# The second transform stage in four quarters of the array: a change to a spectral filter with two dense layers behind it

## The chip, the cores and the metric

The kernel runs on one core of a Trainium2 chip. What counts is the device time of one launch in microseconds (us), the median of several runs. The engines of the core: TensorE (PE; its weight loads are shown as PEld), VectorE (DVE), ScalarE (ACT), GpSimd (POOL, unused here) and SyncE (SP), which issues all transfers.

## The reference

A sequence of 3008 tokens with 256 channels, four batches, all float32, is filtered in the frequency domain and then goes through two dense layers:

```python
X = np.fft.rfft(x, axis=1)                       # x: (4, 3008, 256)
Y = X * (filt_r + 1j * filt_i)[None]             # (1505, 256)
x = np.fft.irfft(Y, n=3008, axis=1).reshape(12032, 256)
r = np.maximum(x @ w_in, 0.0); x = (r * r) @ w_out          # 2048 wide
g = x @ w_gate; silu = g / (1.0 + np.exp(-g))
out = (silu * (x @ w_val)) @ w_out2                          # 1536 wide
```

## The kernel before

**The transform** is split as 3008 = 64 x 47 (and uses the 24 + 24 real rows that 47 folds to). Stage A is a product with a 128 x 128 matrix ("psA", input "x0", "x1" or "xin", stored to the DRAM tensor s1 of its batch). Stages B and C work on 16 *slots* of a batch. A slot is 96 rows (two sets of 48) by 2 x 256 columns: stage B multiplies it by the 96 x 96 block matrix of two 48 x 48 transforms ("psB"), VectorE multiplies the result by the complex filter (lines 519, 524 twice, and 536, which adds the two parts "t1" and "t2"), stage C multiplies by the inverse block matrix ("psC"), ScalarE copies it out and it is stored to s2. Slot 0 is special: real and imaginary rows mix, and it needs four matrices for every product, over 256 columns each. Stage D ("psx", line 790) takes s2 back to tokens and is the entrance of the dense layers.

**Two ways of multiplying float32.** In batch 0, and in batch 1's stage A, matmuls take whole float32 operands (lines 645, 671, 678, 731, 790). Everywhere else both operands are split into two float32r parts and a product is three matmuls (`product`, lines 365 to 367: low x high, high x high, high x low); ScalarE makes the high part (a cast, line 353) and VectorE the low part (a subtraction, line 357). For stages B and C of batches 1 to 3 that means two splits per slot (`fsplit`), and the split matrices of slot 0 lie in DRAM ("sc") and are fetched per batch ("sp").

**Where the pieces run.** `first_ab` does batch 0 ahead of everything else, since nothing can start without it: stage A, stages B and C (`inverse`), batch 1's stage A, then stage D for the first 1024 tokens. Batches 1 to 3 are cut into steps by the generator `stages_ab`, one `yield` each, and a step is called now and then between the products of the dense layers (`side`). The dense layers ("psh", "pA" to "pC", "gA" to "gC", "vA" to "vC", "psg", "psv", and "acc" for the second product of a layer) are over 9,000 matmuls on 128 x 128 blocks over 416 to 512 columns.

**The order** of each engine's instructions is fixed when the program is built. Each step is handed to a `Plan` with an engine, a cost in us that its author wrote down, a rank (its place in the text plus a bias) and the tiles it uses; `emit` plays the steps through, takes on each engine the one that can begin first by these costs (the lower rank within 0.12 us), and gives tiles to buffers. `Buffers` gives its buffers in the order in which the tiles were declared, so that a tile that can't have one yet holds back those behind it; the ones marked loose don't keep that order. On the chip each engine then runs its list strictly in that order and waits where data isn't there yet. The pools that matter here: `pool_f`, 12 buffers of 2 KB a row for the inputs, filters, split parts and outputs of stages A to C; `pool_bank`, four banks of the matmul output memory; `pool_z`, 14 buffers of 4 KB a row, which hold batch 0's inputs "b0" and filters "f0".

Of the kernel before, what the change touches and what calls it, by code (L numbers as in the profile page):

```python
# [21 lines left out]
NQ = 16  # L22
# [20 lines left out]
def _constants():  # L43
# [34 lines left out]
    z = np.zeros((48, 48))  # L78

    def two(x, y):  # L80
        m = np.zeros((96, 96))
        m[:48, :48], m[48:, 48:] = x, y
        return m

    def quarter(i, j, x):
# [11 lines left out]
    mats = [  # L97
        two(t, t), two(ti, ti),
        two(rr, t), two(mr, z), two(rm, z), two(mm, t),
        two(irr, ti), two(imr, z), two(irm, z), two(imm, ti),  # L100
    ]
    cm = np.zeros((96, 10, 96), np.float32)
    for i, m in enumerate(mats):
        cm[:, i] = m
# [62 lines left out]
class Plan:  # L167
# [39 lines left out]
    def emit(self):  # L207
# [22 lines left out]
        def begin(s):  # L230

            at = base[s.i]
            for t in s.tiles:
                if t.slot is None:
# [3 lines left out]
                    best = min((b.free[k] for k in t.among), default=None)  # L238
# [59 lines left out]
def fft_conv_moe_kernel(ctx, tc, x, filt, amat, cmat, sgn, w1, w2, wg, wv, wo, out):  # L298
# [6 lines left out]
    plan = Plan()  # L305
    add = plan.add
# [3 lines left out]
    sc = dr.tile([96, 2, 8, 96], F32, name="sc", tag="sc")  # L310
# [11 lines left out]
    pool_f = Buffers(sb, "f", 12)  # L322
    pool_d = Buffers(sb, "d", 4)
    pool_sp = Buffers(sb, "sp", 1)
# [6 lines left out]
    ch = sb.tile([96, 2, 96], F32R, name="ch")  # L331
    cl = sb.tile([96, 2, 96], F32R, name="cl")
    sg = sb.tile([96, 2, NQ], F32, name="sg")
# [166 lines left out]
    def by_slot(s):  # L500
        return s.rearrange("(r e) n d -> r (e n) d", e=4)

# [6 lines left out]
    def filtered(p, f, ff, q, t1, t2, engine):  # L509


        def pv():
            return p.t[:96].rearrange("p (c d) -> p c d", c=2)

        def cd(t):
            return t.t[:96].rearrange("p (c d) -> p c d", c=2)

        dve(
            lambda: nc.vector.tensor_tensor(cd(t1), pv(), ff()[:, 0:1, :].to_broadcast([96, 2, D]), op=ALU.mult),
            [p, f], [t1],  # L520
        )
        for c in range(2):
            dve(
                lambda c=c: nc.vector.scalar_tensor_tensor(
                    cd(t2)[:, c, :], pv()[:, 1 - c, :], sg[:, c, q:q + 1], ff()[:, 1, :], op0=ALU.mult, op1=ALU.mult
                ),
                [p, f, "sg"], [(t2, c)], cost=0.42,
            )
        if engine == "POOL":
            add(  # L530
                "POOL", 1.45, lambda: nc.gpsimd.tensor_tensor(t1.t[:96], t1.t[:96], t2.t[:96], op=ALU.add),
                [t1, (t2, 0), (t2, 1)], [t1],
            )
        else:
            dve(
                lambda: nc.vector.tensor_tensor(t1.t[:96], t1.t[:96], t2.t[:96], op=ALU.add),
                [t1, (t2, 0), (t2, 1)], [t1],
            )

    def stages_ab(b):  # L540
# [22 lines left out]


        v1, v2 = by_slot(s1[b]), by_slot(s2[b])

        def slot_product(p, m, q, hi, lo, special):
            if q:
                product(
                    p, lambda: p.t[:96], ["ch"], lambda: (ch[:, m, :], cl[:, m, :]),  # L570
                    [hi, lo], lambda: (hi.t[:96], lo.t[:96]), 546,
                )
                return
            for c in range(2):
                for s in range(2):
                    product(
                        p, lambda c=c: p.t[:96, c * D:(c + 1) * D],
                        [special], lambda i=2 * c + s: (special.t[:, 0, i, :], special.t[:, 1, i, :]),
                        [hi, lo], lambda s=s: (hi.t[:96, s * D:(s + 1) * D], lo.t[:96, s * D:(s + 1) * D]),
                        256, start=s == 0, stop=s == 1,  # L580
                    )

        def load_special(m):
# [654 lines left out]
```

## Time and profile before

| | |
|---|---|
| median of 3 runs | 2275.01 us (2273.07 to 2275.43) |
| the profiled execution | 2271.08 us, of which the span of its instructions is 2269.3 us |
| TensorE, busy | 2244.5 us, 99% |
| VectorE, busy | 1712.0 us, 75% |
| ScalarE, busy | 1381.1 us, 61% |

The profile is one execution. A matmul's record is longer than its distance to the next one, since matmuls overlap at their ends; how long something occupies TensorE is read from start to start. Every name in a row ("psB", "fhi") is a tile with its buffer number left out; a tile that is written by one of several wrappers shows under the name that the helper gave it. A whole float32 matmul leaves two records.

### The profile page before, as it was taken

The numbers are of one execution on the slowest core, as the hardware profiler recorded it, in microseconds if no ns is written. First come the engines' busy times: TensorE is split into PE (matmuls) and PEld (weight loads), VectorE is DVE, ScalarE is ACT, GpSimd is POOL, SyncE is SP. The second block draws the span as 40 slices with busy tenths as digits, with TensorE's granted clock in tenths as the row PEclk, the third lists the DMA queues.
The fourth block names the chain that finished last, engine by engine and source line by source line (L and its number), as shares of the span: only waits on it lengthen the run. The fifth ranks groups of instructions, "written<-read, shape, count | busy, mean of one in ns | idle before, by whom it ended". The sixth has DMA issues, their size and how long they took to land.

```text
span 2269.3 us, 28911 instructions
## 1 busy us (share of the span) xinstructions
PE 2244.5 (99%) x10142; PEld 1855.8 (82%) x10142; DVE 1712.0 (75%) x2844; ACT 1381.1 (61%) x2464; POOL 0.2 (0%) x4
## 2 busy tenths in 40 slices
PE   6999999999999999999999999999999999999999
PEld 2688888888888887888888888888888888889889
DVE  3898898887678888667787787766776766767765
ACT  2788655565665656666566665655555655555655
POOL 0000000000000000000000000000000000000000
PEclk8999999999999999999999999999999999999999
DMA  9987768655765555656454555454454454445453
GB/s 287 361 284 258 251 238 278 214 187 194 241 206 164 165 175 187 209 200 218 158 164 141 188 184 167 166 179 163 153 172 131 156 180 160 160 153 169 153 190 135
DMA packets 201425, 439.03 MB, mean 193 GB/s; under 512 B 18080, under 2 KB 110496, under 8 KB 201280
## 3 DMA queue, kind: packets, MB, share of 16 engines
q1 hardware_dynamic: 201280, 437.18, 58.2%
q8 instruction: 80, 1.31, 0.2%
q14 instruction: 65, 0.53, 0.1%
HBM read 365.48 MB, written 71.63 MB: 193 GB/s over the span
## 4 chain that ended last, share of the span: by engine, by line
PE 96%; DMA 3%; ACT 0%; DVE 0%; issue 0%; SPq 0%; ACTq 0%
PE acc L365 13%; PE acc L367 13%; PE acc L366 13%; PE pA L365 3%; PE pA L366 3%; PE pA L367 3%; PE gA L365 3%; PE vA L365 3%; PE vA L367 3%; PE vA L366 3%; PE gA L366 2%; PE gA L367 2%; PE psx L790 2%; PE pC L365 2%; PE pC L367 2%; PE pC L366 2%
## 5 line engine op out<-in xcount | busy, mean ns | idle before, releaser
L367 PE MATMUL acc<-glo,ws 128*128 128x512 f32 (+2 forms) x1280 | 492.6, 385 | 0.0
L365 PE MATMUL acc<-ghi,ws 128*128 128x512 f32 (+2 forms) x1280 | 492.6, 385 | 0.0
L366 PE MATMUL acc<-ghi,ws 128*128 128x512 f32 (+2 forms) x1280 | 492.4, 385 | 0.0
L357 DVE TENSOR_TENSOR glo<-v,ghi 128x512 fp32r<-128x512 f32 (+2 forms) x438 | 291.8, 673 | 88.3 <-ACT ghi L353 83.9
L353 ACT CAST ghi<-v 128x512 fp32r<-128x512 f32 (+2 forms) x438 | 264.2, 610 | 125.0 <-DVE v L967 70.5
L365 PEld LDWEIGHTS acc<-ghi,ws 128*128 128x128 f32 x1280 | 240.2, 188 | 44.8
L367 PEld LDWEIGHTS acc<-glo,ws 128*128 128x128 f32 x1280 | 240.2, 188 | 44.8
L366 PEld LDWEIGHTS acc<-ghi,ws 128*128 128x128 f32 x1280 | 240.3, 188 | 44.5
L955 ACT COPY v<-pA 128x512 f32<-128x512 f32 (+2 forms) x240 | 138.3, 576 | 153.6 <-PE pA L367 149.4
L955 ACT COPY v<-vA 128x512 f32<-128x512 f32 (+2 forms) x198 | 114.2, 577 | 117.0 <-PE vA L367 112.3
L955 ACT COPY v<-gA 128x512 f32<-128x512 f32 (+2 forms) x198 | 114.1, 576 | 98.5 <-PE gA L367 95.2
L961 DVE TENSOR_TENSOR v<-vC,v 128x512 f32<-128x512 f32 (+2 forms) x132 | 89.6, 679 | 110.5 <-ACT v L955 109.6
L961 DVE TENSOR_TENSOR v<-pC,v 128x512 f32<-128x512 f32 (+2 forms) x160 | 108.3, 677 | 70.5 <-ACT v L955 40.7
L967 DVE SCALAR_TENSOR_TENSOR v<-v 128x512 f32<-128x512 f32 (+2 forms) x240 | 156.2, 672 | 2.4
L961 DVE TENSOR_TENSOR v<-gC,v 128x512 f32<-128x512 f32 (+2 forms) x132 | 89.5, 678 | 89.1 <-PE gC L367 74.3
L981 ACT ACTIVATE v<-v 128x512 f32<-128x512 f32 (+2 forms) x198 | 123.3, 623 | 50.5 <-DVE v L961 49.8
L987 DVE TENSOR_TENSOR v<-v 128x512 f32<-128x512 f32 (+2 forms) x198 | 133.0, 674 | 2.9
L357 DVE TENSOR_TENSOR glo<-r,ghi 128x512 fp32r<-128x512 f32 (+2 forms) x144 | 95.7, 676 | 4.9 <-ACT ghi L353 4.9
L353 ACT CAST ghi<-r 128x512 fp32r<-128x512 f32 (+2 forms) x144 | 88.4, 614 | 12.7 <-PE acc L366 9.2
L974 ACT ACTIVATE r<-pA 128x512 f32<-128x512 f32 (+2 forms) x80 | 47.0, 588 | 80.5 <-PE pA L367 79.9
L365 PE MATMUL pA<-z,wa 128*128 128x512 f32 (+2 forms) x240 | 93.0, 387 | 0.6 <-ACT v L955 0.6
L366 PE MATMUL pA<-z,wa 128*128 128x512 f32 (+2 forms) x240 | 92.3, 385 | 0.0
(224 smaller groups left out, 4735.7 us busy)
## 6 DMA issues: line engine op xcount, KB each, us to landing
wa<-dc SPq DMA_DIRECT2D x212, 512.0 KB, 3.5
ws<-ds SPq DMA_DIRECT2D x160, 512.0 KB, 4.4
wb<-db SPq DMA_DIRECT2D x212, 384.0 KB, 5.1
db<-po SPq DMA_DIRECT2D x20, 512.0 KB, 5.9
wa<-db SPq DMA_DIRECT2D x20, 512.0 KB, 4.7
dc<-po SPq DMA_DIRECT2D x20, 512.0 KB, 4.9
bin<-s SPq DMA_DIRECT2D x48, 192.0 KB, 5.6
fil<-in_filt SPq DMA_DIRECT2D x48, 192.0 KB, 5.5
```

Of the source, the lines that this page charges most:

```text
L353: act(lambda: nc.scalar.copy(fhi(), fsrc()), [src], [hi], n, psum, rank)
L357: lambda: nc.vector.tensor_tensor(flo(), fsrc(), fhi(), op=ALU.subtract), [src, hi], [lo], n, rank=rank
L365: nc.tensor.matmul(p, wl, mh, start=start, stop=False, skip_group_check=True)
L366: nc.tensor.matmul(p, wh, mh, start=False, stop=False, skip_group_check=True)
L367: nc.tensor.matmul(p, wh, ml, start=False, stop=stop, skip_group_check=True)
L790: nc.tensor.matmul(o.t[:, begin - n * w:end - n * w], x3[i // 5].t[:, i % 5, 128 * h:128 * h + 128], ai[:, first + begin - lo:first + end ...
L955: act(lambda: nc.scalar.copy(v.t[:, :w], p.t[:, :w]), [p], [v], w, True, URGENT)
L961: lambda: nc.vector.tensor_tensor(v.t[:, :w], p.t[:, :w], v.t[:, :w], op=ALU.add), [p, v], [v], w, rank=URGENT
L967: lambda: nc.vector.scalar_tensor_tensor(h.t[:, :w], h.t[:, :w], 0.0, h.t[:, :w], op0=ALU.max, op1=ALU.mult),
L974: act(lambda: nc.scalar.activation(h.t[:, :w], p.t[:, :w], AF.Relu), [p], [h], w, True, URGENT)
L981: lambda: nc.scalar.activation(t.t[:, :w], src.t[:, :w], AF.Silu), [src], [t], w, psum, URGENT if psum else 0
L987: lambda: nc.vector.tensor_tensor(g.t[:, :w], g.t[:, :w], src.t[:, :w], op=ALU.mult), [g, src], [g], w,
```

## The change

Two slots form a *pair*, eight pairs a batch. A pair's input is loaded so that the first set of 48 rows of both slots lies in rows 0 to 47 and the second in rows 64 to 111, the slots side by side in the columns; one instruction now multiplies 48 rows by a matrix of 64 columns in one quarter (64 x 64) of the array. `quarters` writes the four matmuls of a product, one per quarter, in turn: two row groups (output bank 0 and 1) times two column groups (output partitions 0 to 63 and 64 to 127). Each streams 512 columns of whole float32; for pair 0, which holds slot 0, the first quarter takes four matmuls over 256 columns instead. This is done in all four batches, so that the splits of stages B and C, the "sc" tensor and the "sp" tiles go. The outputs of a product lie in two banks, each of which is filtered on its own over 128 rows.

In batch 0 line 536's addition is left out (`added` is False): "t1" and "t2" both go into the product of stage C, which is then eight matmuls (for pair 0, fourteen). In batches 1 to 3 the addition stays.

Pair inputs and evicted pairs of all batches ("bin" in batches 1 to 3, "eb") share a new pool of two buffers, `pool_e`; `pool_f` goes from 12 to 9, and batch 1's "e1" moves to `pool_h`. A pair is loaded by two transfers of 192 KB, stored by two; a slot's filter comes in two pieces of 64 rows, 16 of them unused. The eleven matrices `cm` stay in a tile of their own, and the signs are loaded in four pieces and set out by two copies. The planner takes two tiles of one pool in one step into account.

The core of the diff:

```diff
-    cm = np.zeros((96, 10, 96), np.float32)
+    mats = [t, ti, rr, mr, rm, mm, irr, imr, irm, imm]
+    cm = np.zeros((128, 11, 64), np.float32)
     for i, m in enumerate(mats):
-        cm[:, i] = m
+        cm[:48, i, :48] = m
+    cm[64:112, 0, 16:] = t
+    cm[64:112, 1, :48] = ti
+    cm[16:64, 10, :48] = cm[80:, 10, :48] = ti
...
-    pool_f = Buffers(sb, "f", 12)
+    pool_f = Buffers(sb, "f", 9)
     pool_d = Buffers(sb, "d", 4)
-    pool_sp = Buffers(sb, "sp", 1)
+    pool_e = Buffers(sb, "e", 2)
...
+    def quarters(o, fo, fs, m, i, r):
+        def fn():
+            res, src = fo(), fs()
+            streams = []
+            for g in range(2):
+                for k in range(2):
+                    shift = m == 1 and k == 1
+                    rows, cols = slice(64 * g, 64 * g + (64 if shift else 48)), slice(64 * k, 64 * k + 64)
+                    last = len(src[k]) - 1
+                    q = []
+                    for c in range(2):
+                        for n, d in enumerate(src[k]):
+                            if i or g or k:
+                                if c == 0:
+                                    w = cm[rows, 10 if shift else m, :]
+                                    q.append((res[g][cols], w, d[rows], n == 0, n == last))
+                            else:
+                                for s in range(2):
+                                    w = cm[rows, 2 + 4 * m + 2 * c + s]
+                                    first = s == 0 and n == 0
+                                    q.append((res[g][cols, c], w, d[rows, s], first, s == 1 and n == last))
+                    streams.append(q)
+            while any(streams):
+                for q in streams:
+                    if q:
+                        p, w, d, start, stop = q.pop(0)
+                        nc.tensor.matmul(p, w, d, start=start, stop=stop, skip_group_check=True)
+        add("PE", (0.95 if i else 1.4) * (2 if len(r) > 4 else 1), fn, list(r) + ["cm"], o)
...
+    def inverse(b, i, ys):
+        o = [bank("psC") for _ in range(2)]
+        quarters(
+            o, lambda: [cd(p) for p in o], lambda: [[cd(y) for y in t] for t in ys], 1, i,
+            [y if n == 0 else (y, c) for t in ys for n, y in enumerate(t) for c in range(2 if n else 1)],
+        )
+        e = Tile(pool_e, [128, 2, 2, D], F32, "eb")
+        for j in range(2):
+            act(
+                lambda j=j: nc.scalar.copy(e.t[:, j].rearrange("p c d -> p (c d)"), o[j].t), [o[j]], [(e, j)], psum=True
+            )
...
-        for q in range(NQ):
-            pair = step_b(q)
+        ready = [("s1", b, g) for g in range(NG)]
+        for i in range(NP):
+            xb = Tile(pool_e, [128, 2, 2, D], F32, "bin")
+            keys = load_pair(s1[b], ready, xb, i, -60)
+            fs = [Tile(pool_f, [128, 1, 2 * D], F32, "fil") for _ in range(2)]
+            fkeys = load_filter(fs, lambda k, fs=fs: fs[k].t, i, -60)
+            o = [bank("psB") for _ in range(2)]
+            quarters(
+                o, lambda o=o: [cd(p) for p in o], lambda xb=xb: [[xb.t[:, j]] for j in range(2)], 0, i, keys
+            )
             yield
-            step_c(q, *pair)
+            ys = []
+            for k in range(2):
+                t1, t2 = narrow(pool_f, "t1"), narrow(pool_f, "t2")
+                filtered(o[k], fkeys[k], lambda f=fs[k]: f.t[:, 0].rearrange("p (c d) -> p c d", c=2), i, k, t1, t2, True)
+                ys.append([t1])
+                yield
+            inverse(b, i, ys)
             yield
```

What the lists of the engines look like at three places. **TensorE, a "psB" product of batch 1 between products of the dense layers,** before ("acc" is a second-layer product, "psv" a first-layer one):

```order
L366 MATMUL psv<-z,wa 128x512
L367 MATMUL psv<-z,wa 128x512
L365 MATMUL psB<-fhi,cl 96x512
L366 MATMUL psB<-fhi,ch 96x512
L367 MATMUL psB<-flo,ch 96x512
L365 MATMUL acc<-ghi,ws 128x512
L366 MATMUL acc<-ghi,ws 128x512
```

and now (a row of x4 is four equal rows, one per quarter; a whole float32 matmul is one row here):

```order
L362 MATMUL acc<-ghi,ws 128x512
L363 MATMUL acc<-glo,ws 128x512
L534 MATMUL psB<-bin,cm 64x512 x4
L361 MATMUL psg<-z,wa 128x512
L362 MATMUL psg<-z,wa 128x512
```

Three matmuls for one slot stood there, four matmuls for two slots stand there now. **TensorE, the last "psC" products of batch 0,** before, with batch 1's stage A ("psA") between and behind them:

```order
L671 MATMUL psC<-t_489,cm 96x512
L731 MATMUL psA<-x_400,am 128x512
L671 MATMUL psC<-t_502,cm 96x512
L731 MATMUL psA<-x_400,am 128x512
L731 MATMUL psA<-x_410,am 128x512 x2
```

and now (t_574 and t_582 are "t1" of the pair's two sets, t_577 and t_587 "t2"):

```order
L743 MATMUL psA<-x_459,am 128x512
L534 MATMUL psC<-t_574,cm 64x512
L534 MATMUL psC<-t_582,cm 64x512
L534 MATMUL psC<-t_574,cm 64x512
L534 MATMUL psC<-t_582,cm 64x512
L534 MATMUL psC<-t_577,cm 64x512
L534 MATMUL psC<-t_587,cm 64x512
L534 MATMUL psC<-t_577,cm 64x512
L534 MATMUL psC<-t_587,cm 64x512
L743 MATMUL psA<-x_459,am 128x512
```

One matmul per slot has become eight per pair, four for each part of the filtered value. **SyncE, from batch 0's last store (s_0_67 is s2 of batch 0) to the load of stage D (x_559 before, x_693 now),** before:

```order
L691 DMA s_0_67<-e_524 96x2x256
L736 DMA s_1_64<-e_527 128x512
L736 DMA s_1_64<-e_540 128x512
L458 DMA dw_98<-wa 128x512
L736 DMA s_1_64<-e_543 128x512
L773 DMA x_559<-s_0_67 128x1280
```

and now:

```order
L603 DMA s_0_67<-eb 48x4x256 x2
L748 DMA s_1_64<-e_639 128x512
L748 DMA s_1_64<-e_652 128x512
L748 DMA s_1_64<-e_658 128x512
L748 DMA s_1_64<-e_661 128x512
L748 DMA s_1_64<-e_674 128x512
L748 DMA s_1_64<-e_676 128x512
L463 DMA ds_136<-po 128x1024
L748 DMA s_1_64<-e_680 128x512
L883 DMA wa<-db_77 128x1024
L777 DMA x_693<-s_0_67 128x1280
```

Between the store and the load stood four transfers, and now there are nine.

## Rows read from the trace of the kernel before

**Rows 1.** The page: busy us of each engine, busy tenths of TensorE in 40 slices, its granted clock, and the chain that ended last by engine.

```profile
PE 2244.5 (99%) x10142; PEld 1855.8 (82%) x10142; DVE 1712.0 (75%) x2844; ACT 1381.1 (61%) x2464; POOL 0.2 (0%) x4
PE   6999999999999999999999999999999999999999
PEclk8999999999999999999999999999999999999999
PE 96%; DMA 3%; ACT 0%; DVE 0%; issue 0%; SPq 0%; ACTq 0%
```

**Rows 2.** Stretches: us from the span's start, length, then busy us of each engine with its instructions, the granted clock of TensorE, the busy share of the DMA engines, GB/s.

```profile
23.00:53.00 30.00, 23.79 (x50) 9.27 (x50) 17.46 (x34) 4.73 (x8) 0.00 (x0) 0.76 1.01 257
53.00:72.00 19.00, 17.70 (x32) 5.60 (x32) 18.66 (x36) 5.38 (x9) 0.00 (x0) 0.82 0.94 346
86.00:2269.00 2183.00, 2177.42 (x9979) 1827.54 (x9977) 1663.66 (x2752) 1349.92 (x2410) 0.00 (x0) 1.00 0.57 189
```

**Rows 3.** TensorE in order of time (start, us, what): a "psB" product of batch 1, and the first matmul of a special one with the first matmul behind it.

```profile
348.14 0.40 PE L365 MATMUL psB<-fhi,cl 96*96 96x512 f32 x1
348.37 0.40 PE L366 MATMUL psB<-fhi,ch 96*96 96x512 f32 x1
348.61 0.39 PE L367 MATMUL psB<-flo,ch 96*96 96x512 f32 x1
348.84 0.39 PE L365 MATMUL psg<-z,wa 128*128 128x512 f32 x1
...
196.93 0.28 PE L365 MATMUL psB<-fhi,sp 96*96 96x256 f32 x1
...
198.34 0.39 PE L365 MATMUL acc<-ghi,ws 128*128 128x512 f32 x1
```

**Rows 4.** Groups of TensorE's matmuls and weight loads by form: count, busy us, mean ns of one, idle before.

```profile
L365 PE MATMUL psC<-fhi,cl 96*96 96x512 f32 x45 | 18.1, 402 | 0.0
L365 PE MATMUL psB<-fhi,cl 96*96 96x512 f32 x45 | 17.9, 399 | 0.0
L671 PE MATMUL psB<-b,cm 96*96 96x512 f32 x30 | 19.8, 755 | 3.2 <-DVE t L524 3.1
L367 PE MATMUL psB<-flo,sp 96*96 96x256 f32 x12 | 3.4, 281 | 0.0
L365 PEld LDWEIGHTS acc<-ghi,ws 128*128 128x128 f32 x1280 | 240.2, 188 | 44.8
```

**Rows 5.** TensorE in order of time in batch 0: whole float32 products of stages B and C, two records each, and the first ones behind a wait.

```profile
42.48 0.59 PE L671 MATMUL psB<-b,cm 96*96 96x512 f32 x1
42.91 1.07 PE L671 MATMUL psC<-t,cm 96*96 96x512 f32 x2
43.83 1.02 PE L671 MATMUL psB<-b,cm 96*96 96x512 f32 x2
44.69 1.07 PE L671 MATMUL psC<-t,cm 96*96 96x512 f32 x2
...
54.30 1.99 PE L671 MATMUL psB<-b,cm 96*96 96x512 f32 x2 [3.09 <-DVE t L524]
```

**Rows 6.** TensorE in order of time: a whole float32 "psx" group between products of the dense layers.

```profile
290.22 0.39 PE L367 MATMUL acc<-glo,ws 128*128 128x512 f32 x1
290.45 1.05 PE L790 MATMUL psx<-ai,x 128*128 128x96 f32 x8
291.25 0.48 PE L365 MATMUL psg<-z,wa 128*128 128x512 f32 x1
291.57 0.40 PE L366 MATMUL psg<-z,wa 128*128 128x512 f32 x1
```

**Rows 7.** The chain of waits ahead of the dense layers, in order of time (start, us, what it was).

```profile
44.14 8.55 DMA b<-s
52.69 0.68 DVE t L519
...
61.42 0.86 PE psB L671 x2
62.27 0.91 PE psC L671 x2
...
72.08 0.59 ACT e L689
...
81.37 4.65 PE psx L790 x40
86.02 0.28 PE psh L365
```

**Rows 8.** VectorE in order of time, batch 0's filter (line 519, 524 twice, 536); in brackets its idle time and what ended it.

```profile
52.69 0.69 DVE L519 TENSOR_TENSOR t<-psB,f 96x512 f32<-96x512 f32 x1 [4.65 <-DMA b<-s]
53.30 0.86 DVE L524 SCALAR_TENSOR_TENSOR t<-psB,sg,f 96x256 f32<-96x256 f32 x2
54.19 0.69 DVE L536 TENSOR_TENSOR t<-t,t 96x512 f32<-96x512 f32 x1
54.80 0.68 DVE L519 TENSOR_TENSOR t<-psB,f 96x512 f32<-96x512 f32 x1
```

**Rows 9.** ScalarE in order of time, an eviction of "psC" in batch 0.

```profile
55.59 0.58 ACT L689 COPY e<-psC 96x512 f32<-96x512 f32 x1 [5.53 <-DMA s<-e]
```

**Rows 10.** Transfers issued from 18 to 60 us: count, KB each, median us from issue to landing.

```profile
b<-s SPq DMA_DIRECT2D x8, 384.0 KB, 9.6
f<-in_filt SPq DMA_DIRECT2D x7, 384.0 KB, 10.4
s<-e SPq DMA_DIRECT2D x9, 192.0 KB, 6.6
```

**Rows 11.** The same from 90 us on.

```profile
bin<-s SPq DMA_DIRECT2D x48, 192.0 KB, 5.6
```

More of the change, by code (lines that the diff above doesn't have):

```diff
@@ L237, in begin @@
                         return None
-                    best = min((b.free[k] for k in t.among), default=None)
+                    n = held.count(b)
+                    held.append(b)
+                    best = sorted(b.free[k] for k in t.among)[n]
                     if best == float("inf"):
@@ new lines, in by_pair, with load_pair @@
+    def by_pair(s, i, k):
+        return s.rearrange("(q c k e) n d -> k (e n) (q c) d", c=2, k=2, e=2)[k, :, 4 * i:4 * i + 4]
+    def load_pair(s, r, t, i, rank, last=()):
+        for k in range(2):
+            dma(
+                lambda k=k: nc.sync.dma_start(
+                    t.t[64 * k:64 * k + 48].rearrange("p j c d -> p (j c) d"), by_pair(s, i, k)
+                ),
+                r, [(t, k)] + (list(last) if k else []), 192, rank,
+            )
+        return [(t, 0), (t, 1)]
@@ L562, in stages_ab @@
             yield
[L565 to L581, printed above, removed]
@@ L653, in first_ab @@
             )
-        dma(lambda: nc.sync.dma_start(cm.t, cmat), [], [cm], 360)
-        dma(lambda: nc.sync.dma_start(sg, sgn), [], ["sg"], 12)
+        dma(lambda: nc.sync.dma_start(cm, cmat), [], ["cm"], 352)
+        signs = Tile(pool_h, [128, 2, 2, NQ], F32, "signs")
+        for j in range(2):
+            for k in range(2):
+                dma(
+                    lambda j=j, k=k: nc.sync.dma_start(signs.t[64 * j:64 * j + 64, k], sgn[32 * k:32 * k + 64]),
+                    [], [(signs, j, k)], 3,
+                )
+        for j in range(2):
+            p = slice(64 * j, 64 * j + 64)
+            act(
+                lambda j=j, p=p: nc.scalar.copy(
+                    sg[p].rearrange("p k c i -> p (k c) i"),
+                    signs.t[p].rearrange("p k c (i j) -> p j (k c) i", j=2)[:, j],
+                ),
+                [(signs, j, 0), (signs, j, 1)], ["sg"], 32,
+            )
         dma(lambda: nc.sync.dma_start(ai, amat[:, 1, :]), [], ["ai"], 64)
@@ new lines, in first_ab @@
+        ys = {}
+        for i in range(NP + 1):
+            if i < NP:
+                if i % 2 == 0:
+                    fb = [Tile(pool_z, [128, 2, 2 * D], F32, "f0") for _ in range(2)]
+                    fkeys = load_filter(fb, lambda k, fb=fb: fb[k].t, i, 0)
+                xb = Tile(pool_z, [128, 2, 2, D], F32, "b0")
+                keys = load_pair(s1[0], ready, xb, i, 0, ["b0 read"] if i == NP - 1 else [])
+                o = [bank("psB") for _ in range(2)]
+                quarters(
+                    o, lambda o=o: [cd(p) for p in o], lambda xb=xb: [[xb.t[:, j]] for j in range(2)], 0, i, keys
+                )
+                ys[i] = []
+                for k in range(2):
+                    t1, t2 = narrow(pool_f, "t1"), narrow(pool_f, "t2")
+                    filtered(
+                        o[k], fkeys[k],
+                        lambda fb=fb, i=i, k=k: fb[k].t[:, i % 2].rearrange("p (c d) -> p c d", c=2), i, k, t1, t2, False,
+                    )
+                    ys[i].append([t1, t2])
+                if i in (0, 1, 3, 5):
@@ L775, in load_x @@
                     ),
-                    [("s2", b, q) for q in range(NQ)], [t] + (["b0 done"] if c == 0 and i else []), 128 * len(of),
+                    [("s2", b, i, k) for i in range(NP) for k in range(2)], [t] + (["b0 done"] if c == 0 and i else []), 128 * len(of),
                 )
```

161 lines of the change are left out of this document (38 added, 123 removed).

## Prediction

> **What bounds the kernel now.** I read the page first, then the stretches, then single matmuls, then the start. The page says it at once: TensorE is busy for 2244.5 of 2269.3 us, every slice from the second on is full, and the chain that ended last is 96% TensorE [rows 1]. The stretches say where it is not so: from 86 us to the end TensorE is busy for 2177 of 2183 us at the full clock, and only ahead of 86 us are there holes [rows 2]. So two questions are enough. After 86 us: how many nanoseconds of TensorE does the changed stage take? VectorE and ScalarE (1664 and 1350 us busy of 2183) have room, and work taken from them there buys nothing. Ahead of 86 us: what sets the moment at which the first "psh" product begins?
>
> In the second stretch one "psB" or "psC" product of a slot is three matmuls at distances of 0.23 us: from 348.14 to 348.84, that is 0.70 us. The special product of slot 0 (twelve matmuls over 256 columns) lasts from 196.93 to 198.34, 1.41 us [rows 3]. The counts by form, 45 per matmul of the three and 12 of a special one, say 45 "psB" and 45 "psC" products and three special ones of either [rows 4]. **The stage costs 90 x 0.70 + 6 x 1.41 = 71.5 us of TensorE in batches 1 to 3.** That is the most the change could give back there.
>
> **The change part by part.** *Products after 86 us.* 96 products become 48 groups: 42 of four matmuls over 512 columns, and 6 (pair 0, forward and back, three batches) of seven, of which four over 256 columns share one quarter. These are whole float32. What such a matmul costs alone is in batch 0: fifteen products left thirty records [rows 4], so one is two records, 0.43 us apart (42.48 to 42.91), and the next product starts 0.86 us after it (43.83 to 44.69) [rows 5]. The length follows the 512 columns; 48 rows instead of 96 change nothing in it. What the trace of before does not show is four of them in four quarters. From below: all four side by side, 0.86 us. From above: one after the other, 4 x 0.86 = 3.44 us. The two ends lie on both sides of the 2 x 0.70 = 1.40 us that a pair costs now, so this one value decides the case. I take the lower end, because quarters on the diagonal share neither rows nor columns of the array, neighbours only one of them, and no two share an output, and because the nearest row, the 0.86 us of rows 5, is a matmul that occupies the array for the whole of its stream with at most 96 of its rows and columns in use. It is a choice, not a reading, and the rivals are built on it.
>
> To that come the edges of a group. Going into whole float32 from the three-part products costs nothing in the "psx" groups (0.23 us from the last "acc"), coming out costs 0.32 instead of 0.23 us [rows 6]. I take 0.09 us for each of the two edges of a group: 0.86 + 0.18 = 1.04 us. The group of seven is as long as its quarter with four halves, 4 x 0.43 = 1.72, and 1.90 with the edges. Sum: 42 x 1.04 + 6 x 1.90 = 55.1 us, **16.4 us less than 71.5**. Without edges it is 46.4 (25.1 less). If at each edge the array first has to run empty (a matmul's record is 0.39 us long at a distance of 0.23, so 0.16 [rows 3]) and then load weights in the open (0.19 [rows 4]), an edge costs 0.35, the groups 1.56 and 2.42, the sum 80.0: 8.5 us more than now. These are the ends of this term.
>
> The Trainium skill, TensorEngine Tiling (Array Packing), Key Properties, has a rule on each side: tiles work independently of each other, and a change of the tiling mode drains the engine. The rows show no change of the tiling mode. By the second rule, with the 0.16 us of the record's tail at each edge, the group would cost 1.18 us and the gain shrink from 16.4 to about 10 us.
>
> *Loads after 86 us.* Pair data and evicted pairs now share two buffers in strict turn, so a pair's load can be asked for only when the pair before is being evicted. At the closest place the order leaves 18 matmuls, some 4 us, and the group itself between "psC" of one pair and "psB" of the next; the load of 192 KB takes 5.6 us [rows 11]. Where the distance is 30 matmuls or more, it is hidden. Two or three of the 24 pairs are closer: **+2 us**, from 0 to +8 if more loads are late. While it waits, all of TensorE's queue stands behind that matmul.
>
> *Work that goes.* Per pair 4 casts and 4 subtractions; the filter's steps and the evictions stay in number and go over 128 rows, no longer for it. All of it lies beside a full TensorE: 0. A slot's filter load of 192 KB becomes two pieces of 128 KB, a third more bytes: 0 after 86 us, where the DMA engines are busy for 57% [rows 2].
>
> *Batch 0, ahead of 86 us.* VectorE paces it: a slot takes 2.11 us (52.69 to 54.80), and the sum that goes is 0.61 of it (54.19 to 54.80) [rows 8]. Over 16 slots that is 9.8 us. But VectorE also sat idle for 4.65 us until a transfer ended, and ScalarE's eviction waited 5.53 us until 55.59 for a store that gave its buffer back [rows 8, 9]: in this stretch the DMA engines are busy without a break, and 10 us pass between asking and landing [rows 2, 10]. What is late next is this. The change adds 1 MB of filter bytes (4.1 us at 257 GB/s), and evictions get two buffers where they had a share of twelve: two pairs per round of two copies each (2 x 0.58), issue and landing (6.6), some 8 us, so 4 us a pair against 2 x 1.77 us now (a "psB" and "psC" row of rows 7). From the landing at 52.69 on, six pairs need two whole rounds before the last pair is copied, at about 70; now that copy began at 72.08 [rows 7]. So about -2 us. Behind it the order moves: six stores of batch 1 and a weight load now stand between batch 0's last store and the load that "psx" needs, where two or three stores stood. Each of these stores waits for an eviction of a "psA" product of 0.86 us: +4 us. TensorE then idles ahead of "psx"; after the 3.09 us of idleness at 54.30 it ran at 1.2 GHz, 1.99 us where 1.02 is usual [rows 5], so +2 us for "psx" (4.65 us [rows 7]) at that clock. Together **+4 us**. The ends: -5 (the sums of the eight slots after 52.69 in full, nothing late) and +14 (a third round of 8 us on top, and 2 us more at the low clock).
>
> *The sum.* -16.4 + 2 + 4 = -10.4 us. The profiled execution took 2271.08, so 2260.7; the median of the runs lies 3.9 us above the profiled one, so **2264.6 us**. With the ends of the terms, of which not all come together, 2252 to 2283.
>
> **The rivals.** *In order, half by half (slower).* A whole float32 matmul is two records, and the second needs the same quarter as the first. If TensorE begins matmuls only in the program's order, the first half of the next quarter has to stand behind the second half of this one. Then only neighbours overlap: four matmuls are five halves, 5 x 0.43 = 2.15, 2.33 with edges; the seven come to 2.79 + 0.18 = 2.97. Stage: 42 x 2.33 + 6 x 2.97 = 115.7, +44.2 us. Batch 0 then needs (5 + 9) x 0.43 = 6.0 us a pair, 48 us from 27.3 on, to 75.5: +3.5, and +4 behind it. Sum about +51: **2326 us**, 2312 to 2342. It decides from 48g = 66.3, a group of 1.38 us, upwards. For it: the records of all products follow each other in the program's order [rows 3, 5]. Against it: none of these rows has a free quarter to go to. The Trainium skill, TensorE: Matmul & The Clock Gate, Part 3, states this order: matmuls start and end strictly first in, first out; this speaks for the rival, and no row here tests it with two halves per matmul.
>
> *The quarters don't overlap.* Then a group costs 3.44 + 0.18 and the seven 4.48, 178.9 in all, +107; batch 0 needs 8 x 10.3 us and ends 38 us later. About **2424 us**. For it speaks only that no row shows an overlap.
>
> *The start gives it back (no change).* The groups are short as forecast, but two eviction buffers and the late "psx" load cost the upper end of 14 us: -16.4 + 14 + 2 = -0.4, **2274.6 us**. It decides from 14 us of delay at 86 us.
>
> **How the numbers follow.** Chances: forecast 0.46, in order 0.36, start 0.10, no overlap 0.08. A measurement of this kernel can tell 0.2%, 4.5 us, from no change. Of the forecast 0.38 lies below 2270.5, 0.06 within and 0.02 above; of the start 0.02, 0.06 and 0.02; the other two are slower. Faster 0.40, same 0.12, slower 0.48: the likeliest single case is a gain, though losses in all weigh a little more. For 8 in 10 the range must take in most of the in-order case: 2252 to 2335 leaves out 0.05 below and some 0.14 above.
>
> **What would show it.** A group's first matmul to the next product's first: 1.0 us is the forecast, 2.3 the order, 3.6 no overlap; the starts of its eight records say which (all first halves within some tens of ns, or in steps of 0.43). The entry and exit distances against 0.23 give the edges. The first "psh" at 86 to 100 us gives the start, DMA as releaser of "psB" after it the late loads. I am wrong if a group costs over 1.4 us.

## The result and the profile after

The changed kernel takes 2290.09 us (median of 4 runs, 2286.8 to 2295.89), the kernel before 2274.04 in the runs beside it: a ratio of 1.008 with an interval of 1.0065 to 1.0095, 0.8% slower. The profiled execution took 2295.89 us (span 2294.1), the longest of the four; that matters below, where its 25 us are larger than the 16 us of the medians.

The stretches of the changed kernel (columns as in [rows 2]), with a cut at its first "psh" product:

```profile
23.00:53.00 30.00, 19.56 (x98) 8.24 (x98) 13.90 (x29) 2.90 (x5) 0.00 (x0) 0.65 1.09 230
53.00:72.00 19.00, 12.13 (x74) 3.75 (x74) 8.01 (x17) 4.92 (x9) 0.00 (x0) 0.73 1.05 295
72.00:86.00 14.00, 12.34 (x60) 4.33 (x57) 11.69 (x24) 8.47 (x16) 0.00 (x0) 1.00 0.96 337
86.00:111.00 25.00, 9.99 (x48) 7.99 (x48) 5.13 (x9) 6.40 (x12) 0.00 (x0) 0.66 0.99 339
111.00:2294.00 2183.00, 2174.79 (x10057) 1788.93 (x10056) 1612.11 (x2652) 1299.85 (x2312) 0.00 (x0) 1.00 0.57 187
```

The first "psh" product starts at 110.84 instead of 85.83 us. From there to the end it is 2183.2 us, before 2183.4. So the whole loss of this execution is the start, and the main part, which was to give 14.4 us, gave 0.2. Two questions follow: what holds the start up, and where did the groups' gain go?

**The groups.** TensorE in order of time around one group of batches 1 to 3, which answers to [rows 3]; the two rows behind the dots are the same group in two narrow windows, so that its records come apart:

```profile
373.91 0.39 PE L363 MATMUL acc<-glo,ws 128*128 128x512 f32 x1
374.23 1.09 PE L534 MATMUL psB<-bin,cm 48*64 48x512 f32 x8
375.25 0.50 PE L361 MATMUL psg<-z,wa 128*128 128x512 f32 x1
375.59 0.39 PE L362 MATMUL psg<-z,wa 128*128 128x512 f32 x1
...
374.23 0.66 PE L534 MATMUL psB<-bin,cm 48*64 48x512 f32 x4
374.71 0.61 PE L534 MATMUL psB<-bin,cm 48*64 48x512 f32 x4
```

Four matmuls leave eight records: four start together at 374.23 (within 20 ns in the records), four together at 374.71. So the quarters run side by side, and the halves don't stand in the program's order. The group lasts 1.02 us to the next product (375.25), the distance into it is 0.32 (373.91 to 374.23) and the one behind it 0.34 us, where 0.23 is usual. Its whole price is 1.02 + 0.09 + 0.11 = 1.22 us.

The weight loads of the same stretch show where a group differs from other products:

```profile
373.69 0.19 PEld L363 LDWEIGHTS acc<-glo,ws 128*128 128x128 f32 x1
374.23 0.21 PEld L534 LDWEIGHTS psB<-bin,cm 48*64 48x64 f32 x8 [0.35 <-issue]
375.25 0.19 PEld L361 LDWEIGHTS psg<-z,wa 128*128 128x128 f32 x1 [0.81 <-ACT po L349]
```

Between products of the full array a load starts 0.22 us ahead of its matmul (373.69 for 373.91). The group's first load starts only with the group (374.23), and the first load behind it only with its product (375.25). It is so, within 31 ns, in all 48 groups: no load crosses an edge of a group.

**The start.** The chain that ended last in the changed kernel, which answers to [rows 7]:

```profile
66.35 8.05 DMA s<-eb
74.50 0.59 ACT eb L599
...
77.28 1.72 PE psC L534 x16
79.00 1.91 PE psA L743 x4
80.92 1.88 PE psC L534 x16
82.79 3.65 PE psA L743 x8
...
96.51 7.37 DMA x<-s
...
104.01 7.02 PE psx L794 x40
```

The last "psC" ends at 82.79 us (before 72.04), "psx" begins at 104.01 (before 81.37) and takes 7.02 instead of 4.65 us. Between the two stands SyncE's queue. What it issued there (start, us, what):

```profile
82.80 1.02 SPq L603 DMA_DIRECT2D s<-eb  x2
83.91 0.62 SPq L748 DMA_DIRECT2D s<-e  x1
84.58 0.70 SPq L883 DMA_DIRECT2D wa<-db  x1
85.37 0.60 SPq L748 DMA_DIRECT2D s<-e  x1
86.07 0.43 SPq L454 DMA_DIRECT2D dw<-wa  x1
86.59 0.43 SPq L458 DMA_DIRECT2D db<-po  x1
87.11 2.44 SPq L603 DMA_DIRECT2D s<-eb  x2
89.65 4.50 SPq L748 DMA_DIRECT2D s<-e  x6
94.24 0.51 SPq L463 DMA_DIRECT2D ds<-po  x1
...
95.37 1.08 SPq L883 DMA_DIRECT2D wa<-db  x1
96.51 1.25 SPq L777 DMA_DIRECT2D x<-s  x2
```

The last pair's stores go out at 87.11 and 88.08 us, and nine transfers that have nothing to do with them stand ahead of the load that "psx" needs ("x<-s", 96.51).

From the last "psC" to "psx" there are four steps. The second store is issued 5.3 us after the product (before 0.6), lands 6.0 us later (2.5), the load is issued 2.4 us after that (0.4) and takes 7.4 us (5.6). So of the 11.9 us by which this gap grew, 4.6 stand ahead of the store (0.5 of it a second copy by ScalarE, the rest the queue), 3.5 are its landing, 2.0 are the nine transfers behind it, and 1.8 are the load.

**The main part.** What TensorE waited for after 111 us, and the longest of these places:

```profile
PE psB L534 <- DMA bin<-s: 2.6, 4, 1.7
PE psv L361 <- DMA wa<-db: 1.3, 1, 1.3
```

```profile
1104.55 1.07 PE L534 MATMUL psB<-bin,cm 48*64 48x256 f32 x4
1107.35 1.52 PE L534 MATMUL psB<-bin,cm 48*64 48x512 f32 x10 [1.73 <-DMA bin<-s]
1108.80 0.56 PE L361 MATMUL pC<-z,wa 128*128 128x512 f32 x1
1109.15 0.63 PE L362 MATMUL pC<-z,wa 128*128 128x512 f32 x1
```

This is a group of seven. Its first two matmuls (four records) run, and the data of the next ones, the other half of the pair, isn't there. The group lasts 4.25 us instead of 1.87, and the products behind it are at distances of 0.35 and then 0.43 instead of 0.23 us: the granted clock is 0.74 in the stretch of 1106.5 to 1112 us and 0.50 (1.2 GHz) from 1109.2 to 1112.1.

### The profile page after: what moved, and what is told of

Same layout as the page of the kernel before. It is cut to its first block, busy times and chain, and to the rows that moved or that the text cites. A ratio compares the mean times of both kernels' runs of the same rounds, so it can differ in the third digit from the quotient of the medians.

```text
span 2294.1 us, 29073 instructions
## 1 busy us (share of the span) xinstructions
PE 2242.1 (98%) x10354; PEld 1818.5 (79%) x10354; DVE 1651.1 (72%) x2730; ACT 1331.5 (58%) x2368; POOL 0.2 (0%) x4
## 4 chain that ended last, share of the span: by engine, by line
PE 93%; DMA 5%; DVE 1%; SPq 1%; ACT 0%; issue 0%; ACTq 0%; DVEq 0%
PE acc L361 13%; PE acc L363 13%; PE acc L362 13%; PE pA L361 3%; PE pA L363 3%; PE pA L362 3%; PE gA L361 3%; PE gA L363 3%; PE gA L362 3%; PE vA L361 3%; PE vA L363 2%; PE vA L362 2%; PE psx L794 2%; PE pC L361 2%; PE pC L363 2%; PE pC L362 2%
```

## The experiments

Theories on the start. 1: batch 0 is held up by its two eviction buffers, and behind it by the places in SyncE's queue. 2: the DMA engines are full (a share of 1.0 in every stretch to 111 us), above all with 1 MB more of filter rows, and no order helps. 3: TensorE itself: the doubled products of batch 0, the half clock, and, in a later form, what stands between the groups in its queue. The table holds the marks of every run that goes with the start (us, from the time lines; the last column is the ratio of the runs to those of the kernel before on the same chip):

| run | last pair landed | last "psC" ends | "psx" begins | first "psh" | from there to the end | ratio |
|---|---|---|---|---|---|---|
| before | 57.03 | 72.04 | 81.37 | 85.83 | 2183.4 | 1 |
| after | 66.24 | 82.79 | 104.01 | 110.84 | 2183.2 | 1.0080 |
| four eviction buffers | 63.21 | 79.93 | 100.46 | 106.71 | 2179.8 | 1.0072 |
| load first | 60.24 | 76.95 | 90.45 | 96.92 | 2182.4 | 1.0027 |
| both | 62.93 | 79.78 | 92.51 | 99.05 | 2182.8 | 1.0038 |
| addition back | 60.83 | 86.68 | 102.55 | 109.72 | 2180.8 | 1.0090 |
| both, 48 filter rows | 61.25 | 77.70 | 90.17 | 96.82 | 2180.7 | 1.0024 |
| both, "psA" last | 59.49 | 69.28 | 87.86 | 95.50 | 2178.9 | 1.0023 |
| all of these | 58.90 | 65.85 | 86.46 | 93.35 | 2180.2 | 1.0014 |
| and filters later | 56.77 | 65.54 | 86.72 | 93.12 | 2178.9 | 1.0010 |
| and weights later | 55.68 | 62.37 | 80.04 | 86.26 | 2182.7 | 0.9978 |
| batch 0 as before | 57.14 | 73.58 | 84.28 | 88.73 | 2178.3 | 1.0002 |
| the same, two load buffers | 57.62 | 77.46 | 86.77 | 92.86 | 2181.3 | 1.0020 |

One caution: the run with doubled groups (below) has the changed kernel's instructions ahead of "psh" unaltered, and there the last pair landed at 60.50, "psC" ended at 77.15 and "psh" began at 104.57. So one and the same start differs by 6 us between executions, with the landing of the loads; a difference of 3 us in one profile tells nothing. Steadier is the time from that landing to the end of the last "psC": 16.6 and 16.7 us in these two.

**Four eviction buffers.**

```diff
-        e = Tile(pool_e, [128, 2, 2, D], F32, "eb")
+        e = Tile(pool_e if b else pool_big, [128, 2, 2, D], F32, "eb")
```

> Batch 0's evicted pairs get four buffers instead of the two that they share in the changed kernel; nothing else moves. Theory 1 (two eviction buffers hold batch 0 up: ScalarE waits 3 to 11 us per round for stores): the last psC of batch 0 ends some 8 to 11 us earlier than at 82.7 us; how much of that reaches the first psh (110.84 us) depends on the load ahead of psx, so psh at 100 to 106, total 2280 to 2286. Theory 2 (the DMA engines are saturated by the extra filter bytes, whatever the buffers): ScalarE's waits move to other waits, psh stays within 3 us of 110.8, total 2288 to 2292. Theory 3 (the doubled products of batch 0 and the half clock set the pace): no change either.

Median 2289.86 us, as before the edit. In the changed kernel the view of waits has ScalarE's "eb" waiting for stores; here it waits for the products instead:

```profile
ACT eb L599 <- PE psC L534: 25.4, 7, 9.1
```

(in the changed kernel "ACT eb L599 <- DMA s<-eb" is 18.0 us at three places). The wait was there and was worth nothing: the last "psC" came 2.9 us earlier, inside the 6 us that executions differ by, and 16.7 us after the last landing, as in the changed kernel. This half of theory 1 falls.

**The load of the third stage first.** Batch 1's "psA" loop is written behind the third stage's first loads, which now write a key that batch 1's stores read:

```diff
-                    [e], [("s1", 1, 2 * i + j)], 256,
+                    [e, "x3 asked"], [("s1", 1, 2 * i + j)], 256,
```

> The loads of the third stage's input are queued right behind batch 0's last stores, ahead of batch 1's first stores, the weight load and the filter-bank loads that stand there in the changed kernel. Theory 1 (the place in SyncE's queue makes 8 to 10 of the 21 us from the last psC to psx): the gap falls to 10 to 14 us, psh at 101 to 104, total 2280 to 2284. Theory 2 (saturated DMA engines): the load is asked for earlier and takes as much longer, the gap stays at 18 us or more, psh at 108 or later. Theory 3: gap unchanged but for the half clock, psh at 109 or later.

Median 2280.17, ratio 1.0027 (1.0014 to 1.0039): 10 us of the 16. From the last "psC" to "psx" it is 13.5 instead of 21.2 us. The places in SyncE's queue were the largest part of the loss, by the order alone: no byte and no product differs. The last store still takes 6.5 us to land, with nothing behind it; in the runs with the old batch 0 below, whose stores have the old form, it is 2.2 and 2.1 us. Why the new stores land later wasn't tried.

**Both edits.** 

> Four eviction buffers and the early place of the load together. Theory 1: both gains add, psh at 90 to 95 us against 110.84, total 2271 to 2276. Theory 2: psh at 105 or later. Theory 3: psh at 108 or later.

Median 2280.76, "psh" at 99.05. The gains don't add, since one of them is none. None of the three theories had this number; 13 us of the start stay open.

**The addition comes back.**

```diff
-  filtered(o[k], fkeys[k], ..., i, k, t1, t2, False)
-  ys[i].append([t1, t2])
+  filtered(o[k], fkeys[k], ..., i, k, t1, t2, True)
+  ys[i].append([t1])
```

> VectorE's addition comes back in batch 0 (two tiles per slot added as in the kernel before), and batch 0's psC groups have half as many matmuls. Theory 1: VectorE and the smaller products are both beside the waits for stores and loads, so psh moves by no more than 3 us either way (108 to 114), total 2287 to 2294. Theory 3 (the doubled products at the half clock cost the start): batch 0's last psC ends 5 us or more earlier, psh at 106 or earlier.

Median 2292.26, no gain. The last "psC" ends 25.9 us behind the last pair's landing instead of 16.6, but the sum alone doesn't explain it: with the edit the planner also moved TensorE's queue.

```profile
67.96 6.74 PE L743 MATMUL psA<-x,am 128*128 128x512 f32 x8 [0.67 <-ACT e L746]
79.90 0.69 DVE L544 TENSOR_TENSOR t<-psB,f 128x512 f32<-128x512 f32 x1 [6.06 <-PE psB L534]
```

Twelve "psA" products of batch 1 now stand ahead of batch 0's last "psC" from 65.2 us on, where five stood, and VectorE, which has the sum to do, sat idle for 6.06 us until a "psB" behind seven of them had run. "psh" is where theory 1 has it (109.72), but as the order moved, the run tells neither what the sum is worth nor what the doubled products cost: both stay open.

**48 filter rows.** On top of both edits, batch 0 loads only the rows that a quarter uses; GpSimd zeroes the spare ones before:

```diff
-  view(k)[64 * j:64 * j + 64], filt[32 * k:32 * k + 64]...
+  view(k)[64 * j + 16 * k:][:48], filt[48 * k:][:48]...
```

> The kernel of both edits (four eviction buffers, early load), with batch 0's filter loads cut to the 48 rows of a quarter that are used, so 1 MB of transfers is gone ahead of the third stage; the 16 spare rows are filled with zeros by GpSimd before. Theory 2 (the DMA engines set the pace: the last pair of batch 0 landed at 62.9 us with 64 rows, at 57.0 in the kernel before): the last pair lands 3 to 4 us earlier and the first psh comes 3 to 4 us earlier, at about 95 against 99.05. Theory 1 (what is left is the order of the queues): psh stays within 1 us of 99. Theory 3 (TensorE's in-order queue of batch 0, where products of batch 1's first stage stand between the groups): within 2 us of 99.

"psh" at 96.82 against 99.05, ratio 1.0024 against 1.0038. The last pair landed 1.7 us earlier. Not separable from the differences between executions; theory 2, in the form that the extra filter rows are the cause, has at most 2 us. But this profile shows what TensorE stood for:

```profile
63.52 2.05 PE L748 MATMUL psA<-x,am 128*128 128x512 f32 x2 [5.69 <-DMA x<-in_x]
65.50 1.99 PE L534 MATMUL psB<-b,cm 48*64 48x512 f32 x8
```

Its queue is in order, and products of batch 1's first stage stand between the groups of batch 0's last pairs. All pairs had landed by 61.25; the "psB" at 65.50 had to wait behind a "psA" whose x came at 63.4, and both ran at half clock (granted 0.50 from 63.5 to 67.5 us).

**"psA" last.** On top of both edits batch 1's "psA" products read a key, "b0 over", that batch 0's last "psC" group writes:

```diff
-                    0.86, [am, t],
+                    0.86, [am, t, "b0 over"],
```

> The kernel of both edits, with batch 1's psA products put behind the last psC of batch 0 in TensorE's queue (five of them stood between the last three pairs' groups, and their x loads land at 65 to 74 us, after the last pair's data at 63). Theory 3 in its new form (TensorE waits in order for these x loads, 6 us at once): the last psC ends 6 to 8 us earlier, at 72 to 74 against 79.9, and psh comes at 91 to 94 against 99.05, total 2273 to 2276. Theory 2: the tail behind the last pair's landing keeps its 15 us, psh within 2 us of 99.

The last "psC" ends at 69.28 instead of 79.78, 9.8 us behind the last landing instead of 16.9, and earlier than in the kernel before, where "psA" products stand between the last "psC" products too. So this order in TensorE's queue cost batch 0 some 7 us. "psh" gains only 3.5 us of it (95.50): the gap to "psx" grows from 12.7 to 18.6 us, the time goes to the next queue. The theory was right in the place and wrong in what it is worth.

**All of them,** and a pool of one buffer for the pairs' loads of batches 1 to 3:

```diff
-    pool_e = Buffers(sb, "e", 2)
+    pool_e = Buffers(sb, "e", 1)
+    pool_n = Buffers(sb, "n", 1)
...
-            xb = Tile(pool_e, [128, 2, 2, D], F32, "bin")
+            xb = Tile(pool_n, [128, 2, 2, D], F32, "bin")
```

> All edits together: four eviction buffers, early load, 48 filter rows, psA last, and a buffer pool of its own for the pairs' loads of batches 1 to 3, so that a pair's load need not wait for the turn of an eviction. If the start's causes add, psh comes at 87 to 91 us; if the late loads were the turns of two shared buffers, the time from psh to the end falls from 2183 by 4 to 6 us to 2177 to 2179. Total 2264 to 2270, faster than both kernels. If the loads stay late (the turns aren't the cause), 2270 to 2276.

Median 2276.5, ratio 1.0014 (1.0005 to 1.0024): neither of the two forecasts, still slower. Groups that are longer than 1.02 or 1.87 us, since a pair came late, are five in the changed kernel and three in each of the six other runs with shared buffers; here and in the four runs after it with own buffers it is the one of pair 0 of batch 3 (here another one by 0.3 us). TensorE's waits of this run from "psh" on:

```profile
PE psv L362 <- DMA wa<-db: 1.6, 1, 1.6
PE psB L535 <- DMA bin<-s: 1.4, 1, 1.4
```

So the turns of the shared buffers made the others. The one left comes right behind the last store of its batch's first stage, on which its load depends (landed at 1079.40 us, load issued at 1079.42).

**Doubled groups.** Each group of batches 1 to 3 of the changed kernel runs its matmuls twice:

```diff
+            if twice:
+                streams = [q + q for q in streams]
```

> The changed kernel, in which every group of batches 1 to 3 runs its matmuls twice within the group (the output stays what it is). If a group's cost beyond 0.86 us lies at its edges, paid once per group, the second pass costs 0.86 us in the groups of four and 1.72 in those of seven: 42 x 0.86 + 6 x 1.72 = 46.4 us more in all. If it lies in every matmul (quarters hinder each other), the second pass costs as much as the first, 1.22 and 2.07 us: 63.7 us more. If the halves ran in order, half by half, 2.15 and 2.79: 107 us more.

```profile
371.46 0.39 PE L363 MATMUL acc<-glo,ws 128*128 128x512 f32 x1
371.78 1.95 PE L536 MATMUL psB<-bin,cm 48*64 48x512 f32 x16
373.65 0.50 PE L361 MATMUL psg<-z,wa 128*128 128x512 f32 x1
```

A doubled group lasts 1.87 us (371.78 to 373.65) where the single one lasts 1.02: the second pass costs 0.85 to 0.86. So four matmuls side by side cost what one costs, and 1.22 - 0.86 = 0.36 us is paid once per group. (From "psh" to the end it is 2226.8 us in this one execution, 43.6 more; 46.4 was expected. The groups themselves grew by 45.5 us, and the wait for weights at "psv" is gone.)

**Filters later.** On top of all, batch 1's first filter loads read a key of the third stage's loads:

```diff
+  fkeys = load_filter(fs, ..., i, -60, r=["b0 done"] if b == 1 and i == 0 else ())
```

> The kernel of all edits, with the filter loads of batch 1's first pair (four transfers, 512 KB) put behind the third stage's first loads; they stood in SyncE's queue ahead of batch 0's last stores, which were issued 8 us after their data was there. If the queue's places are what is left of the late start: the last stores go out at 69 to 72 instead of 75.2 us, psx begins at 81 to 84 instead of 86.46 and psh at 88 to 91 instead of 93.35; total 2267 to 2273. If the DMA engines' load is what is left, the stores and the loads behind them take as much longer and psh stays at 92 to 94.

Median 2274.23, ratio 1.0010 (0.9999 to 1.0021); "psh" doesn't move. The last stores still go out at 74.27, and SyncE's waits name the reason, a reload of weights that waits until its own store has landed:

```profile
73.84 0.34 SPq L891 DMA_DIRECT2D wa<-db  x1
74.27 0.87 SPq L606 DMA_DIRECT2D s<-eb  x2
...
79.33 0.80 SPq L785 DMA_DIRECT2D x<-s  x2
```

```profile
SPq L891 <- DMA db<-po: 3.8, 2, 3.4
```

**Weights later.** This reload gets the same key:

```diff
-  dma(lambda: nc.sync.dma_start(ta.t..., dblock[i]), [("db", i)], [ta], 512, rank)
+  dma(lambda: nc.sync.dma_start(ta.t..., dblock[i]), [("db", i), "b0 done"], [ta], 512, rank)
```

> The kernel with the filter loads later, in which also the reload of the first weights (wa<-db) is put behind the third stage's first loads. In the run before, SyncE stood for 3.4 us at this reload, until the weights' own store had landed at 73.82 us, with batch 0's last two stores behind it, issued at 74.27 and 74.70. If the queue's places set the start: the last stores go out at 70 to 71.5 us, the third stage's loads at 75.5 to 77 instead of 79.33, psx begins at 83 to 84.5 instead of 86.72, psh comes at 89 to 91 instead of 93.12, total 2267 to 2271, equal to or a little below the kernel before. If the DMA engines' load sets it: the loads behind take longer by what they start earlier, psh at 92.5 to 94. If the weights then come too late, TensorE waits for wa by DMA after psh, by up to 5 us.

```profile
67.47 2.31 SPq L606 DMA_DIRECT2D s<-eb  x3
...
73.50 0.79 SPq L785 DMA_DIRECT2D x<-s  x2
```

Median 2268.68 (2263.9 to 2270.86) against 2273.13 of the kernel before: ratio 0.9978 (0.9968 to 0.9988), the only version that beats both. "psx" begins at 80.04, "psh" at 86.26. Some 3 us of the 6.9 that "psh" gains over the run before are an earlier last "psC" (62.37 against 65.54), which the differences between executions can make; 2.5 us lie between it and the last store, where the reload stood. The profiled execution (2270.75, the second slowest of nine; before 2271.08) doesn't show the gain; the main part there has 2182.7 us, with waits of 1.8 us for weights and 1.6 for pair 0 of batch 3.

**Batch 0 as before,** with its matrices of 96 rows as one more constant, and batches 1 to 3 as in the change with own load and eviction buffers. (Its diff is the kernel before's batch 0, put back.)

> Batch 0 as in the kernel before (96-row products, VectorE's sum, loads of 384 KB, its order of SyncE's queue), batches 1 to 3 as in the changed kernel, with a buffer pool of its own for the pairs' loads there. This is the change's main part alone. If the two parts are independent: psh at 84 to 88 us (85.83 before), and 2179 to 2181 us from there to the end, as in the run of all edits, against 2183.4 before: total 2266 to 2270, 0.1 to 0.2% faster than before. If the main part's gain in the other runs came from work that a late start had already put behind it, the main part takes 2183 or more and the total is 2270 to 2274.

Median 2273.55, ratio 1.0002 (0.9993 to 1.0011). The profile goes nearly as expected (2178.3 us from "psh" on, 5.1 less than before, "psh" 2.9 later), but it is that of the fastest of eleven executions (2268.83), and the median shows no gain. Why this start is 2.9 us late wasn't tried; it has nine common buffers where the kernel before has twelve.

**The same with two load buffers,** seven common ones, and the queue's order of the runs above:

> As the run with the old batch 0, but with two buffers for the pairs' loads of batches 1 to 3 (and seven instead of nine of the common ones; batch 0's evictions go to four buffers that are free then), and with batch 1's first stores and filter loads behind the third stage's first loads in SyncE's queue. If what is left over in the main part (TensorE waited 1.23 us for a pair's load and 1.47 and 1.23 us for weights that stood in SyncE's queue behind a pair's load whose buffer wasn't free) comes from the single load buffer, these waits go, the main part falls from 2178.3 towards the 2175 that 48 groups at 1.22 and 2.07 us give, and psh comes at 84 to 87: total 2262 to 2266. If the waits come from the DMA engines or from the decoding of the weights, the main part stays at 2178 to 2180 and the total at 2266 to 2270. If seven common buffers are too few, psh comes after 89.

Median 2277.23, slower. The waits stay (for weights 3.0 us, for pair 0 of batch 3 1.7), so the single load buffer isn't their cause; its start is the expectation's last case (92.86), though the order of "psA" moved with the buffers. Why the weights come late at "psv", once or twice between 307 and 360 us, in the changed kernel and in most of the runs, as they don't before, stays open.

## Why the prediction was wrong

The forecast was 2264.6, faster; the kernel took 2290.09. In the prediction's terms it was -16.4 + 2 + 4; the profiled execution has about -8 for the groups, nearly +8 for what was late in the main part, and +25 for the start (by the medians the whole loss is 16). The chance of slower, 0.48, was the largest of the three, but lay on the wrong mechanism.

- *Side by side.* Right: 0.86 us for what lies inside, shown by the doubled groups. Both rivals about TensorE (in order half by half, no overlap) fall with the eight records. The Trainium skill, TensorE: Matmul & The Clock Gate, Part 3, says that matmuls start and end in program order. In the groups of four the trace agrees: the four first and the four second halves each come in that order. In the late group at 1104.55 us it doesn't for halves: a second half over 256 columns starts at 1107.63, ahead of those (1107.81 and 1107.84) of two matmuls that stand before its own. Reading from the rule that a second half holds the next quarter's first half was my step, and wrong. The same section has tiles start some 4 ns apart; in the records it is 6 to 7.
- *The edges, 0.09 us each.* This term failed in size; its upper end, 0.35 us an edge, was twice too much. Entry and exit are 0.09 and 0.11 over the usual distance as taken from the "psx" groups; but another 0.16 us lies within the group. 0.36 instead of 0.18 us: 42 x 1.22 + 6 x 2.07 = 63.7, a gain of 7.8 instead of 16.4. The Trainium skill, TensorEngine Tiling (Array Packing), Key Properties, states that a change of the tiling mode drains the engine, and 1.18 us was my sum by it. The trace gives 1.22: I had the better number and set it aside. That the 0.36 us is such a drain no run shows; one load in the open at either edge (records of 0.13 and 0.19 us) would make 0.32, an estimate from those two lengths, and is as near.
- *Late loads, +2 (0 to +8).* Beyond the end. The groups that waited are 6.1 us longer (4.25 instead of 1.87 at 1104.55, and four more), the weights at "psv" took 1.5 (1.71 us from the product before it instead of 0.23) and the half clock behind 1104 us about 1.7, together 9.3. Against the 7.8 that is a loss of 1.5 us; the main part gave 0.2, since waits of 1.7 us for VectorE and ScalarE in the kernel before are 0.7 here and the rest is small. "Two or three of 24 pairs" were five, and a late one can also cost the clock.
- *Batch 0, -2.* The last "psC" came 10.8 us later, not 2 earlier. What the sum that goes is worth here no run shows. The rounds of two buffers, on which I rested the forecast, held nothing up that mattered. What did is not in my list: the last pair lands 9 us later (3.5 in the other execution), of which the extra filter rows have at most 2 and the rest stays open, and TensorE's own queue puts batch 1's "psA" ahead of groups whose data is there, some 7 us by the run with "psA" last.
- *Behind it, +4.* The step that failed most. The gap from the last "psC" to "psx" went from 9.3 to 21.2 us, +12. I had counted what stands behind the last pair's stores (one store of batch 1 too few, and not the store "ds"), and that is 2.0 us of it. I put at nothing what stands ahead of them (stores, filter loads, a reload of weights), 4.6 us, and that they land in 6.0 instead of 2.5 us and the load in 7.4 instead of 5.6. The run with the load first gives 8 us of the gap back by order alone.
- *"psx" at half clock, +2.* Right: 7.02 instead of 4.65, the granted clock 0.66 from 86 to 111 us.
- *The start gives it back.* This rival, at 0.10, is nearest to what happened, with 25 us instead of its 14, and against half the gain, which the late loads took. Its price was bounded by a third round of the eviction buffers, the wrong mechanism.

## What to carry to other kernels

A change that alters loads and buffers on a tuned schedule moves every in-order queue; walk along each queue from the step that ends the stage to the step that needs it, and count what stands in between and what each of those waits for. Where several queues are late by about the same, removing one wait can buy nothing until the others are gone: here seven edits together took the median from 2290.09 to 2268.68 us; the first of them alone gave nothing, the second alone 10 us, and the last one, on top of the others, 5.5. Small products in quarters of the array pay a fixed price per group, so make groups long.

## What the runs showed of the hardware

- Four float32 matmuls over 512 columns in four 64-by-64 quarters cost 0.86 us together, as much as one; a group costs 0.36 us on top, between products of the full array. The weights of a group are not loaded ahead of it, nor those of the product behind it: their first loads start within 31 ns of the first matmul, where between full products a load runs 0.22 us ahead.
- A wait of TensorE in the middle of a group can cost the clock: after the group at 1104.55 us, two of whose seven matmuls ran 2.8 us ahead of the rest (1.73 us of it idle), the products behind were at a distance of 0.43 us for 3.4 us; in the kernel before an idle time of 0.95 us between products of the full array left them at 0.23. The length of the wait alone doesn't decide: the same group waited in all thirteen traces of kernels with groups, and the half clock came behind it in six (idle for 1.36 to 2.14 us) and not in seven (0.58 to 1.66).
- The same start differs between executions by 6 us. The rate of the DMA engines from 23 to 53 us, at a share of 1.0 to 1.1, was 230 GB/s in the changed kernel's profile and 266 in that of the doubled groups, which has the same order of transfers there.
